# Cross-shaped window attention on one core: a newly searched instruction order, three integer and two product buffers, and a start that loads half of x transposed

## The chip, the core and the metric

The kernel runs on one core of a Trainium2 chip. The metric is the device time of one execution in microseconds. TensorE (PE; PEld is its weight load), VectorE (DVE), ScalarE (ACT), GpSimd (POOL) and SyncE (SP) each work through their own list of instructions in order and wait for each other through semaphores.

## What is computed

```python
def reference(x, wqkv, wo):            # x 1x224x224x96, wqkv 96x288, wo 96x96
    qkv = jnp.einsum('bhwc,cd->bhwd', x, wqkv)      # q, k, v: 96 channels each
    # channels 0..47: 28 horizontal stripes of 8 rows x 224 columns = 1792 tokens
    ah = _softmax(jnp.einsum('bqc,bkc->bqk', qh, kh) * scale, axis=-1)
    oh = jnp.einsum('bqk,bkc->bqc', ah, vh)
    # channels 48..95: 28 vertical stripes of 8 columns x 224 rows, the same
    ...
    return jnp.einsum('bhwc,cd->bhwd', o, wo)       # o: both halves side by side
```

So there are 56 attention problems of 1,792 queries by 1,792 keys with 48 channels, and a projection before and behind them.

## The kernel before, in words

**Tiling.** The kernel treats two stripes at a time (a band, `P`, 28 of them: 14 horizontal, then 14 vertical). The two stripes sit side by side in the partitions of TensorE's operands. The 1,792 queries are cut in chunks of 512, 512, 512 and 256 (`CH`). A unit is one chunk against 128 keys (256 for the short chunk), for both stripes: a pair of score matmuls that run at once (L988) fills two PSUM banks with 128 x 1024 scores.

**Two ways to an exponential.** Of the 1,372 units, 1,092 go through ScalarE's Exp, PSUM to a bf16 tile `PT` (L1010). The other 280 (4, 2, 2, 2 a band by chunk, `NDC`) go through integers: VectorE adds a constant and rounds the scores to int16 (`I_sb`, L1048). Two such units make a pair: VectorE masks the pair's fraction into `U_sb` (L1060) and its exponent into `E_sb` (L1062), and the product of `I_sb` and `U_sb`, read as bf16, goes to `G_sb` (L1066). The sum E + G stands for the exponential, so TensorE multiplies both with V. A product of 512 columns is made on POOL, one of 1,024 on VectorE; a bit of the string `far` says which for each half of a pair. Buffers for I and U: `NY` = 2 pairs, for E and G: `NL` = 3 pairs (L396).

**Rest of a band.** TensorE multiplies PT, E and G with V (L941) into one bank per chunk; VectorE copies the finished chunk to `OT_sb` (L904); TensorE multiplies it with wo and a column of ones (L793, L829); VectorE divides by the sums. Horizontal results are staged and moved by DMA to `Ph_sb`, which stays in SBUF; POOL adds vertical results to it (L842), and a DMA writes the output. In between, "fills" make the next band's Q, K (L679) and V (L744) from `xT_sb`, x with channels in the partitions, which transposing DMAs on SP load two bands ahead (`load`, L556).

**What sets the order.** A planner inside the kernel (`Planner`) keeps streams of operations for each engine. It takes the next operation of TensorE, VectorE and POOL from the strings in `PLAN`, a digit for the stream: on TensorE 0 start, 1 scores for ScalarE, 2 scores for VectorE, 3 values times E or G, 4 values times PT, 5 final projection, 6 fill. `bank` gives the PSUM banks. The planner's assumed durations (`ACT` and `SWITCH` at L161 and L162, the numbers handed to `Op` and `fill`) place operations against each other in time, choose free buffers and order SP. They are no instructions; the chip sees only the order and the waits.

**Start.** For band 0, x of both stripes is loaded as plain rows, 112 partitions of 16 tokens (L496; one DMA on SP, one on ACT), turned by 32 matmuls against an identity (`x_turn`, L645) and copied to `xT_sb` (L650). The tokens come out permuted, so the first Q is read in that order (L674) and its copies from PSUM undo it in two strided pieces each (L690, L692). `NWARM` = 6 matmuls on zeros run before that (L524), three more (`warmer`, L757) between the first fills.

Of the kernel before, what the change touches and what calls it, by code (L numbers as in the profile page):

```python
# [24 lines left out]
NDC = [4, 2, 2, 2]  # L25

# [3 lines left out]
        "00000000000000000006000611602106162164144116444123316446121443163124144124143314613413413312416441261341163441"  # L30
        "36312514412316123144414412614411333544146153124164124133361123443134126413411644541135445441441241331241641136"
        "44416451451611333531241644113644125414412414414126133312514414614341612331351241631431341264143116444411464453"
        "13312514412416341154441135443634161541631251431241644112644414412313411344441254134121613331241641341334124164"
        "11354441144544614613313612441541231531144446313641611354451241361612441461241441331241434124154134144125133135"
        "16412316441331641241364116443441213341541245144113644411464464161133344153412514312416412614414412313411364441"
        "44615412316123315314123414312316431164444116445441631313541241631246144115344411633441412631441153461245144124"
        "14414412613331251441461431641233136154123143134126413411644441146543313155414412613412461441136441133444124613"
        "41154461235144124144144126133312514414614316412331361215341431341264134116444411464431335124164145135124414611"
        "36444113344614512315441231612416414414331241341241441631441463135123164144123313441126443146114345414412413314"
        "61244163114644531144361351541236144513126144126144144124154411333541213441441251331234151344133124164113644416"  # L40
        "46146133123514412415311464461134443113464461351241541136446121444126144144412315312315413414441215313312614413"
        "64133121644411364444116446413313451541241631246144113644113344461531241541234164112444164412313311444421451431"
        "21633136124163143153144126341441163444116345315412461441251341134444113364461311544541236144126144126144144123"
        "13411433451241441233154135164123164133412416411364444116444613313412541412431541146344114334611544531612431641"
        "26141241644144123134113455414416412331341261341241531334124164631461411344446155144133124164312416411344441133"
        "54451143641261341261412461441441231341134544124154132133134125144146133136124163114464431461231341146446124135"
        "41146434114633514411364451241354124164121644144121334113344412416412416213313613413312461441135444114464451541"
        "64133135123416412461341154444114633115446344121543412416124164115444213134125133144144126133312416413413314612"
        "44163116445431541214441146444123163411643441154461541336135124413312416124164115444441213313514413461241641233"
        "13164123144313412641341164454113644514414441231631246144114334411633511446345124153412164124164144412133411354"  # L50
        "44124164133134126314412614313314641251341146445415414413413312614412361441163454414133411644612351441531241612"
        "41444164121333154124163144146313125414412413313341241641136444146416413312316412451441136444115446133113544441"
        "26313412614412614414412313411345441241641333141263144126134133412416411364431145334615414124514412316441136444"
        "11463311544541634125134412164124164115444213134125313414414126133312416413413341241641136444114644541631331543"
        "14126414312641441164441331154464515312316124154412414414412613341251331441441136346123415412316413341261441164"
        "44311346335154141246144125134114364441146331154464312514412316412614411444434121353144123144162161333154124163"
        "12461441331541146343114463351544141264144123614411354441143344611164453354124161241541241441641213331541231441"
        "44126313312614416312414363144116444113345331645145144164123145124316411544441163316412531441231641261441154444"
        "12415412335313441116444463312415412416431341361341254133146114644415412441331412641341164454316115444123341641"
        "16345124154312414414123134121633144144126313411644331146335124164311544641531241612514414412416411464453133161"  # L60
        "13544413316441153444126131241644115444412153134125133124144124153131241354431441154444123153135411354415412451"
        "4441125441331145443113544412415414412331541144413341334115434354455"),
    "dve": (
        "00000000000000000003333333332332344323343232442444413232344133233244232344313333232144232333333314423323443333"
        "33313323323442312344333213233442323443333132332334343331333323323442324142133234423234434333333132332344333133"
        "33323324432214432132333334432323344123332334433331332332344232441333321323442323443333331332323443331233332344"
        "23123443332132334423234433313333332323443123333234423123443332132344233234433313323333323443133323323442321442"
        "31333244232333134423323344331333332333234423233144233123344233234433333123323334433133323333244231233442133233"
        "34423234433331333323234431333233244323244132132334432332334431333332323443313333323234423241442133233333442323"
        "44333312332334431333333232344232144333332123442332333314433333232344133333232344232144332132344333232344313233"  # L70
        "32334433331333233234423244412321344232334433333333133232344331333323323234412334442313234423323333331234432344"
        "33333313342323234434123344332132444232333333134432324443133333323323442321443332123442333233333344413232334413"
        "33323333244321323344231323444232344333312323344333314332323442321443332123442323344433331332332344313333332332"
        "32344312344423132344232344333333413323234431433333332323442312344423313323344232334443333133232334431333323323"
        "24431423443213323323443233344433331332323443413333333232344321324443231233244323344433333313332332344313332332"
        "32344343213323344313233444323343233134432323333134433233332344212344423123444333323333333213234323434343433413"
        "433432323443413233243234123434323443432333431333323344323434313342343233444144333313333"),
    "pool": (
        "00000000022122222222222222222222122222222222222222222122222222222222222222212222222222222222212222222222222222"
        "22221222222222222222222221222222222222222222221222222222222222222221222222222222222222222122222222222222222221"  # L80
        "22222222222222222222122222222222222222212222222222222222222212222222222222222222221222222233332222222221222223"
        "32222333332222222222133222222333332222332222132232222333222222222231322223222233322222233222212222223333222222"
        "22223122223222233333222222222212233322333322322223223122223222233332222223322122223223333322322223221222233222"
        "233332233223221332222332222322322322221333333322333333333333332233333"),
    "far": (
        "01001111111111111111111111111111111011111111111111111111111111111111111111111111111111111111111111111111111111"
        "11111111011111111111111111111111111111101111111101111111010110110111111110111111011111011111101111101111011001"
        "110111110111101110101101111110011011110101110000100000000100"),
    "bank": (
        "76547654760127665502475044275047205420540135025320530530404603643064316042064260426426042605326513651365230636"  # L90
# [281 lines left out]
def bass_standalone__window_attn_cswin__vision_kernel(  # L372
# [29 lines left out]
    with es:  # L402
# [234 lines left out]
        def x_cols(c0, c1):  # L637
            return [x_evs[(w, g)] for g in range(4) for w in range(2) if c0 < 4 * XP * (g + 1) and c1 > 4 * XP * g]
# [387 lines left out]
        def add_d(u, soft):  # L1026
# [26 lines left out]
            if j == 0:  # L1053
                return
# [141 lines left out]
```

## Time and profile before

| | us |
|---|---|
| time, median of 3 runs (1023.18 to 1023.66) | 1023.42 |
| profiled execution, its own time | 1023.4 |
| its span, first to last instruction | 1021.6 |
| first exponential starts | 12.32 |
| last exponential ends | 1015.68 |
| busy: TensorE, VectorE, ScalarE, GpSimd | 1001.8, 914.6, 1008.2, 677.6 |

The profile is one execution. Its page gives busy time of each engine, the chain of work that ended last (followed back from the end, at each step to what released it), and groups of instructions with a count, busy time, mean duration and the idle time before them. Matmuls and exponentials are pipelined: one starts before the last has ended, so busy time is a union and the distance from start to start says more than a duration. The timeline lists instructions in order of time, merged where equal ones follow each other, with idle time and its releaser in brackets.

### The profile page before, as it was taken

To read this page: it belongs to the slowest core of one execution; us is meant where nothing else is said; L and a number is where in the kernel's file an instruction comes from. 1 tells how busy PE (TensorE), PEld (TensorE's weight loads), DVE (VectorE), ACT (ScalarE), POOL (GpSimd) and SP (SyncE) were. 2 spreads that over 40 slices of the span, in tenths; PEclk is the share of its full clock that TensorE was granted. 3 is DMA by queue.
4 is the path that set the end of the run, shared out by engine and by line. 5 is a ranking of instruction groups with operands and counts; after the bars stand their busy time and mean duration, and the time that the engine had idled before them with its cause. 6 is when DMAs were issued, how large, how long until landed. Compare 5 with 4: busy or idle time off the path is not lost.

```text
span 1021.6 us, 25550 instructions
## 1 busy us (share of the span) xinstructions
PE 1001.8 (98%) x10681; PEld 387.9 (38%) x10681; DVE 914.6 (90%) x1660; ACT 1008.2 (99%) x1106; POOL 677.6 (66%) x623
## 2 busy tenths in 40 slices
PE   8999999999999999999999999999999999999997
PEld 3333333333333334334333333333333333333333
DVE  8989989988988998898889889989889999998998
ACT  7999999999999999999999999999999999999997
POOL 2667657667756757665677776777677676676534
PEclk9999999999999999999999999999999999999999
DMA  4122443141244342331432212112212222221012
GB/s 103 38 26 41 64 51 42 37 64 29 43 59 48 46 63 39 28 56 31 49 58 47 43 36 56 40 38 45 47 41 42 49 44 46 51 51 33 22 29 48
DMA packets 187915, 46.49 MB, mean 46 GB/s; under 512 B 187576, under 2 KB 187576, under 8 KB 187800
## 3 DMA queue, kind: packets, MB, share of 16 engines
q1 hardware_dynamic: 187432, 44.44, 26.8%
q8 instruction: 83, 1.36, 0.6%
q10 hardware_dynamic: 368, 0.43, 0.1%
q14 instruction: 32, 0.26, 0.1%
HBM read 0.79 MB, written 9.63 MB: 10 GB/s over the span
## 4 chain that ended last, share of the span: by engine, by line
ACT 96%; PE 3%; DMA 0%; DVE 0%; issue 0%; DVEq 0%
ACT PT L1010 96%; PE ps L941 1%; PE ps L988 1%; DMA Ph_sb<-in_x_dram 0%; PE ps L679 0%; PE ps L645 0%; PE ps L829 0%; PE ps L744 0%; DVE out_sb L861 0%; PE ps L757 0%; DVE OT_sb L904 0%; DVE rc L834 0%; PE ps L793 0%; DVEq L402 0%; DVE tmp L838 0%
## 5 line engine op out<-in xcount | busy, mean ns | idle before, releaser
L1010 ACT ACTIVATE PT<-ps 128x1024 bf16<-128x1024 f32 x1092 | 1002.4, 1168 | 1.4 <-PE ps L988 1.0
L1066 POOL TENSOR_TENSOR G_sb<-I_sb,U_sb 128x512 bf16<-128x512 bf16 x472 | 531.3, 1155 | 294.2 <-DVE E_sb L1062 272.5
L988 PE MATMUL ps<-QT_sb,KT_sb 48*128 48x512 bf16 (+1 forms) x3136 | 464.5, 356 | 10.3 <-ACT PT L1010 3.6
L1048 DVE TENSOR_SCALAR I_sb<-ps 128x1024 int16<-128x1024 f32 x280 | 341.6, 1220 | 27.3 <-PE ps L988 21.8
L941 PE MATMUL ps<-PT,V_sb 128*64 128x512 bf16 (+1 forms) x2464 | 364.7, 362 | 0.4 <-ACT PT L1010 0.3
L988 PEld LDWEIGHTS ps<-QT_sb,KT_sb 48*128 48x128 bf16 x3136 | 123.4, 93 | 312.6 <-ACT PT L1010 247.5
L941 PEld LDWEIGHTS ps<-PT,V_sb 128*64 128x64 bf16 x2464 | 118.9, 109 | 113.5 <-issue 90.5
L842 POOL TENSOR_TENSOR out_sb<-tmp,Ph_sb 112x384 bf16<-112x384 f32 x111 | 99.2, 913 | 31.5 <-DVE G_sb L1066 13.8
L941 PE MATMUL ps<-G_sb,V_sb 128*64 128x512 bf16 (+1 forms) x672 | 108.5, 354 | 0.1
L1060 DVE TENSOR_SCALAR U_sb<-I_sb 128x2048 int16<-128x2048 int16 x140 | 99.4, 710 | 0.3
L941 PE MATMUL ps<-E_sb,V_sb 128*64 128x512 bf16 (+1 forms) x672 | 96.2, 354 | 0.8 <-DVE OT_sb L904 0.2
L1062 DVE TENSOR_SCALAR E_sb<-I_sb 128x2048 int16<-128x2048 int16 x140 | 96.4, 688 | 0.0
L679 PE MATMUL ps<-xT_sb,w_sb 96*64 96x512 bf16 x448 | 83.3, 372 | 0.2
L904 DVE CAST OT_sb<-ps 128x512 bf16<-128x512 f32 x112 | 69.6, 621 | 14.5 <-PE ps L941 13.3
L699 DVE TENSOR_SCALAR QT_sb<-ps 128x512 bf16<-128x512 f32 x108 | 66.7, 620 | 16.0 <-PE ps L679 15.3
L705 DVE TENSOR_SCALAR_CACHE_REDUCE KT_sb<-ps 128x512 bf16<-128x512 f32 x110 | 67.7, 619 | 8.4 <-PE ps L679 7.9
L749 DVE CAST V_sb<-ps 128x480 bf16<-128x480 f32 (+1 forms) x112 | 55.8, 501 | 9.5 <-PE ps L744 9.1
L838 DVE TENSOR_TENSOR tmp<-ps,rc 112x384 f32<-112x384 f32 x111 | 61.6, 555 | 2.9 <-DVE rc L834 0.2
L717 POOL TENSOR_SCALAR KT_sb<-KT_sb,negmean 128x1792 bf16<-128x1792 bf16 x27 | 47.5, 1761 | 14.9 <-DVE E_sb L1062 10.9
L800 DVE TENSOR_TENSOR out_sb<-ps,rc 128x384 bf16<-128x384 f32 x98 | 54.5, 556 | 2.9
L941 PEld LDWEIGHTS ps<-G_sb,V_sb 128*64 128x64 bf16 x672 | 34.2, 108 | 44.0 <-issue 32.6
L744 PEld LDWEIGHTS ps<-w_sb,xT_sb 96*64 96x64 bf16 x1568 | 35.9, 112 | 25.9 <-issue 10.0
(45 smaller groups left out, 337.0 us busy)
## 6 DMA issues: line engine op xcount, KB each, us to landing
Ph_sb<-out_sb SPq DMA_DIRECT2D x112, 84.0 KB, 4.4
out_dram<-out_sb SPq DMA_DIRECT2D x111, 84.0 KB, 1.9
xT_sb<-in_x_dram SPq DMA_TRANSPOSE x250, 2.5
Ph_sb<-in_x_dram SPq DMA_DIRECT2D x1, 336.0 KB, 4.7
Ph_sb<-in_x_dram ACTq DMA_DIRECT2D x1, 336.0 KB, 4.9
out_dram<-out_sb ACTq DMA_DIRECT2D x1, 84.0 KB, 2.1
wo_sb<-in_wo_dram SPq DMA_DIRECT2D x4, 9.0 KB
wo_sb<-one_sb SPq DMA_DIRECT2D x4, 0.0 KB
```

What stands on the lines that cost most here:

```text
L679: ins = e.matmul(bk[64 * w:64 * w + 64, 0:qs], lhsT=w_sb[0:C, wblk(P, kind), :], rhs=rhs, start=True, stop=True)
L699: return e.tensor_scalar(dst, src, A128, None, ALU.mult)
L705: return e.tensor_scalar(dst, src, 1.0, None, ALU.mult, ALU.add, accum_out=acc)
L842: return e.tensor_tensor(out_sb[b][0:HB, :, w, 2 * c:2 * c + 2, :].rearrange("p h d c -> p d h c"), tmp[hold[1].tok["t"]][0:HB, 0:n, :].re ...
L904: return e.tensor_copy(OT_sb[b][:, q0:q0 + qs], bk[:, 0:qs])
L941: return e.matmul(bank(k.bank)[64 * w:64 * w + 64, x0:x1], lhsT=lhs(w, kts[i])[p0:p1], rhs=rhs(w, i, qs)[p0:p1, x0:x1], start=(op.tok["fir ...
L988: ins = e.matmul(bank(op.tok["s"][w])[:, i * qs:(i + 1) * qs], lhsT=KT_sb[b][64 * w:64 * w + C2, kt * 128:(kt + 1) * 128], rhs=QT_sb[b][64 ...
L1010: a.fn = lambda e: e.activation(PT[a.tok["p"]][:].rearrange("p (s n) -> p s n", s=2), two(q.tok["s"]), ACTF.Exp, scale=LN128)
L1048: return e.tensor_scalar(dst[:, at:at + 1024].rearrange("p (s n) -> p s n", s=2), two(src), 128.0 * ONE, 0.0, ALU.add, ALU.max)
L1060: f.fn = lambda e: e.tensor_scalar(U_sb[y()][:, :], I_sb[y()][:, :], M_FRAC, HALF, ALU.bitwise_and, ALU.bitwise_or)
L1062: x2.fn = lambda e: e.tensor_scalar(E_sb[x2.tok["l"]][:, :], I_sb[y()][:, :], M_EXP, E_LOW, ALU.bitwise_and, ALU.bitwise_or)
L1066: g.fn = lambda e: e.tensor_tensor(G_sb[x2.tok["l"]][:, i0:i1], I_sb[y()][:, i0:i1].bitcast(BF16), U_sb[y()][:, i0:i1].bitcast(BF16), ALU. ...
```

## The change

The strings of `PLAN` are replaced by others found in a new search; two assumed switch times, the exponential's and several operations' assumed durations change. The pool of integer buffers grows from 2 to 3 pairs and that of products shrinks from 3 to 2. At the start the first stripe's x comes by a transposing DMA on SP straight into `xT_sb`; the second stripe's comes as rows on ACT's queue and is turned by 16 matmuls, whose copies now write the natural order of tokens, so the first Q's copies are plain. All K and Q fills of band 0 wait for both. The weight load moves from SP to ACT's queue. The warm-up matmuls ahead become 9, and two more warmers stand between turning and K. A table of counts by band (`NDP`) is added, empty, and a last unit without a partner could be treated alone.

```diff
@@ planner's figures @@
-SWITCH = {"q": 0.122, "v": 0.097}
-ACT = 0.9165
+SWITCH = {"q": 0.096, "v": 0.097}
+ACT = 0.904
...
-    NPT, NY, NL, NR = 8, 2, 3, 4
-    NWARM, EARLY = 6, 256
+    NPT, NY, NL, NR = 8, 3, 2, 4
+    NWARM, EARLY = 9, 256
...
-        for w in range(2):
-            src = bass.AP(x.tensor, x.offset + w * NTOK * C, [[XJ * C, XP], [1, XJ * C]])
-            op = Op("sp" if w == 0 else "act", 0.65, 3.0, lambda e, w=w, src=src: e.dma_start(xn[0:XP, w, :], src), dma=(s_nat[w], 0))
...
+        x_nat = Op("act", 0.45, 4.1, lambda e: e.dma_start(xn[0:XP, :], src), dma=(s_nat, 0))
+        q_first["act"].append(x_nat)
+        x_tr = Op("sp", 1.3, 5.1, lambda e: e.dma_start_transpose(xT_sb[0][:, 0:1, :], bass.AP(x.tensor, x.offset, [[C, NTOK], [1, 128]])),
+                  dma=(s_x[0][0], 0))
+        q_first["sp"].append(x_tr)
...
-        op_w0 = Op("sp", 0.7, 2.8, lambda e: e.dma_start(w_sb[0:C, :, 0:C2], wqkv.rearrange("c (s d) -> c s d", s=6)), [o_w0], dma=(s_w0, 0))
-        q_first["sp"].append(op_w0)
+        op_w0 = Op("act", 0.7, 3.6, lambda e: e.dma_start(w_sb[0:C, :, 0:C2], wqkv.rearrange("c (s d) -> c s d", s=6)), [o_w0], dma=(s_w0, 0))
+        q_first["act"].append(op_w0)
...
@@ x_turn @@
-                dst, src = xT_sb[0][0:C, w, 4 * g * XP:4 * (g + 1) * XP], bk[0:C, 0:4 * XP]
+                dst = xT_sb[0][0:C, 1, :].rearrange("c (p j) -> c j p", j=XJ)[:, 4 * g:4 * g + 4, :]
+                src = bk[0:C, 0:4 * XP].rearrange("c (j p) -> c j p", j=4)
...
-                on_act = startup and (c < 2 if kind == "q" else c % 2)
+                on_act = startup and (c < 1 if kind == "q" else c % 2)
...
-                    xs = x_cols(0, NTOK) if kind == "q" else x_cols(q0, q0 + qs)
+                    xs = [x_tr] + x_evs
...
-                p, ops = fill(0.43 * qs / 1024, pe_fn, xs + [op_w0], evs, ...
+                p, ops = fill(0.025 + 0.43 * qs / 1024, pe_fn, xs + [op_w0], evs, ...
...
-                p, ops = fill(0.045 * n, pe_fn, (x_cols(k0 * 128, (k0 + n) * 128) if startup else [x_op[(P, w)]]) + [op_w0, o_v1],
+                p, ops = fill(0.0335 * n, pe_fn, ((x_evs if w else [x_tr]) if startup else [x_op[(P, w)]]) + [op_w0, o_v1],
...
-                work = [(t, w, g) for g in range(4) for w in range(2)] + [(k, "k", c) for c in range(NCH)] + [
+                work = [(t, g) for g in range(4)] + [(f, 0), (f, 1)] + [(k, "k", c) for c in range(NCH)] + [
...
```

Of the strings, TensorE's begins with 25 start codes in a row where it began with 19, then a fill and three more. It has 1,092, 280, 560, 1,092, 210 and 329 of the codes 1 to 6, as before; `far` has 242 ones of 280 where it had 236; POOL's has 484 products where it had 472.

## The prediction

> **What bounds the kernel now.** I began with the page. Its first lines show two full engines, its fourth part the chain that ends last, its fifth the groups.
>
> ```profile
> span 1021.6 us, 25550 instructions
> PE 1001.8 (98%) x10681; PEld 387.9 (38%) x10681; DVE 914.6 (90%) x1660; ACT 1008.2 (99%) x1106; POOL 677.6 (66%) x623
> ACT 96%; PE 3%; DMA 0%; DVE 0%; issue 0%; DVEq 0%
> L1010 ACT ACTIVATE PT<-ps 128x1024 bf16<-128x1024 f32 x1092 | 1002.4, 1168 | 1.4 <-PE ps L988 1.0
> L1066 POOL TENSOR_TENSOR G_sb<-I_sb,U_sb 128x512 bf16<-128x512 bf16 x472 | 531.3, 1155 | 294.2 <-DVE E_sb L1062 272.5
> L1060 DVE TENSOR_SCALAR U_sb<-I_sb 128x2048 int16<-128x2048 int16 x140 | 99.4, 710 | 0.3
> L1062 DVE TENSOR_SCALAR E_sb<-I_sb 128x2048 int16<-128x2048 int16 x140 | 96.4, 688 | 0.0
> ```
>
> The reader sees a stream of 1,092 exponentials that carries 96% of the chain, with only 1.4 us of idle in front of them. That hides the real loss, because successive exponentials overlap (1,168 ns each, 1,002 us together). So next I read their starts in the trace: 796 of the 1,091 distances are 904 or 905 ns, the mean is 918.5. **904 ns is the pace of a fed ScalarE; (918.5 - 904) x 1,091 = 15.8 us is lost to scores that come late.** Of it 11.3 us lie in 79 distances over 960 ns, and it is spread evenly: 1.1 to 1.7 us in each 100 us, 2.7 in 900 to 1000.
>
> Then the chain in order of time, for the two ends:
>
> ```profile
> 0.74 4.66 DMA Ph_sb<-in_x_dram
> 5.44 3.22 PE ps L645 x32
> 8.66 1.99 PE ps L679 x8
> ...
> 11.96 0.34 PE ps L988 x2
> 12.32 360.63 ACT PT L1010 x393
> ...
> 988.07 27.61 ACT PT L1010 x30
> ```
>
> The first exponential starts at 12.32 and the last ends at 988.07 + 27.61 = 1015.68. The row of 393 has a pitch of 360.63 / 393 = 0.918.
>
> Last, one stall in the timeline, and the waits:
>
> ```profile
> 906.36 0.63 PE L941 MATMUL ps<-E_sb,V_sb 128*64 128x256 bf16 x8 [0.20 <-ACT PT L1010]
> 906.82 0.34 PE L829 MATMUL ps<-wo_sb,OT_sb 128*64 128x97 bf16 x8
> 906.99 0.38 PE L941 MATMUL ps<-G_sb,V_sb 128*64 128x256 bf16 x4
> 907.31 0.39 PE L988 MATMUL ps<-QT_sb,KT_sb 48*128 48x512 bf16 x2
> 907.74 1.02 ACT L1010 ACTIVATE PT<-ps 128x1024 bf16<-128x1024 f32 x1 [0.52 <-PE ps L988]
> ```
>
> ```profile
> PEld ps L988 <- ACT PT L1010: 247.5, 728, 0.8
> DVE I_sb L1048 <- POOL G_sb L1066: 1.6, 2, 0.9
> ```
>
> The exponential waits because the written order put other matmuls ahead of its scores, not because TensorE has too much to do: score matmuls wait for ScalarE to free a bank 728 times.
>
> **The sum's frame.** Profiled time 1023.4 = 1.8 around the span + 12.32 to the first exponential + 1,091 x 0.904 = 986.3 + 15.8 of stalls + 1.27 (the last exponential) + 5.92 (its end to the span's end). The median shown is 1023.42, the same. The change can touch 12.32, 15.8 and 5.92 only: the number of exponentials (code 1, 1,092 times in both strings) stays.
>
> **Part 1, the start.** Removed: 16 of 32 turning matmuls, 93 ns apart, 1.49 us; four of eight evictions. Moved: the rows now go out on ACT's queue, whose transfer of the same size landed at 5.69, not the 5.40 at which SP's did. So turning runs from 5.73 to 7.22. The first K fill now needs all four turned groups. The fourth group's last matmul starts at 7.13; its eviction on ACT follows as before after 0.335 and takes 0.54: 8.00, so K starts at about 8.06, not 8.59 (two new warm-ups, 2 x 0.427 from 7.22, fill this wait). The transposing DMA of the other half sits first on SP: the first such transfer here took 5.55 from issue to landing, so 0.74 + 5.55 = 6.3, behind cover. At the late end it lands at 7.7, as the first one does now, and still hides. Ahead of it on SP the row transfer goes away; behind it the two transposes for the second band slide by about a microsecond at most and have until 14 us. The weight load moves to ACT's queue behind the rows and ahead of the table load: issued at about 1.4, and at SP's 4.6 us it lands near 6.0, before 8.06; the 1.28 us table load slides by some 0.7 into time when ACT idles until 6.46.
>
> From the first K fill to the first score took 11.89 - 8.59 = 3.30. Its string now holds all 25 start codes ahead of the first score: behind q come warm-up, V, warm-up, V, warm-up with pitches 0.38, 0.32, 0.43, 0.32, 0.43, and 0.32 to the score, 2.20, on top of 1.325 from K to q. That is 3.53: first score at 11.59, first exponential 0.43 later, 12.02, a gain of 0.30. At this part PE's pace matters: matmuls of 512 columns stand 427 ns apart until about 9.5 us and 213 to 225 later (the granted-clock column reads 1.00 throughout, so the pitches are what tells). The warm-up grows from 6 to 9 (9 x 0.427 from 1.19 reaches 5.03), so the idle stretch shrinks from 1.5 us to under 1. If PE is at its fast pace by 5.7, turning saves 0.75 and the fills 0.6 more; then the evictions (2.75 from K to the corrected keys) bind, and the exponential comes at 10.7. The other bound is a late strided eviction or weight load: 13.3. The strided eviction itself is priced by L690, 0.39 for 256 strided columns, against 0.38 for dense ones on L704: nothing. I take 11.7, nearest to the 12.02, so **-0.6**.
>
> The Trainium skill, "TensorE: Matmul & The Clock Gate", section "What's actually happening", says that about 3.4 us of sustained work in a free-running window releases the full clock. The trace's switch near 9.5, 4.1 us after work resumed at 5.44, fits it. By the rule alone the 3.84 us of warm-up may or may not do it, and the start would be 10.7 or 12.0.
>
> **Part 2, the order of the stream.** Count the strings. Both have 1,372 score pairs (codes 1, 2), 1,652 value products (3, 4), 210 finals (5), 329 fills (6). The switches between score and value work rise from 1,838 to 1,915. By pitches in the trace: 0.2165 per score pair, 0.226 per value product, 0.17 a final, 0.208 a fill, 0.098 a switch (305 to 312 instead of 213): 954.6 us before, 962.2 after. Per exponential 0.874 and 0.881, both under 0.904. So 77 switches cost 7.5 us of TensorE, covered as long as TensorE has 22 us to spare.
>
> Why then 15.8 of stalls? The order was laid out for an exponential every 0.9165 (ACT, L162) with a switch of 0.122 to scores and 0.045 per V block. The chip runs at 0.904, so ScalarE outruns the order by 0.0125 x 1,091 = 13.6 us, and has to be stopped for it; what is left, 2.2, is the order's own. The new string is laid out for 0.904, a switch of 0.096 and V blocks of 0.0335, which are what the trace measures (93 to 104 ns; 0.030 to 0.034). So the 13.6 can go. It won't go whole: the hidden margin between planned and real TensorE work sinks from some 37 us (992 by the old figures against 955) to 10 (972 against 962), so a wait that used to be swallowed now reaches ScalarE. Bounds for the stalls: 2.2 and 15.8. I take **6**, in the half nearer to 2.2, since the 13.6 has a cause that goes: **-9.8**.
>
> **Part 3, products and buffers.** far has 242 ones for 236: six halves move from DVE (0.695 each, -4.2 us of 914.6) to POOL (12 x 1.155 = +13.9 of 677.6). Neither engine is full. From the write of E to the last read of its pair takes 6.8 us in the middle and 11.3 at most; two buffers would have been free at least 2.8 us before their next use, so the third product buffer did nothing: 0. The integer pair lives 10.6, at most 16.5, and two buffers came free 0.1 to 0.7 us ahead in the tight places, with the 1.6 us of waits shown above; a third takes these away. DVE is not on the chain, so I count 0 and leave the gain in the 6.
>
> **Part 4, the rest.** The end: behind the last score the new string has two value products, then two finals at the very end as before: 5.92 stays. The empty table of counts and the case of a lone unit do nothing (ten units in each band, always paired). Sum: 1.8 + 11.7 + 986.3 + 6 + 1.27 + 5.92 = **1013.0**.
>
> **Rivals.**
> *Stalls come back elsewhere.* TensorE has less slack, and where 25 exponentials in a row hold over 0.904 of its work each (4% of stretches before, 9% after) they stall anyway; only the start gains. Stalls 15 to 17: 1022 to 1024, say 1023. For it: even now PE is at 98%. Against: no stretch of 100 exceeds 0.90.
>
> *Slower: products arrive late on POOL.* Place: the G reads in TensorE's queue, which end only 1.25 us (median) after the last product; behind them wait the next scores. U's operation takes 661 to 695 ns alone, but up to 1,321 where a POOL operation lies beside it (25 of 140 have one). With more on POOL in a shorter span (691 + 99 + 96 + 26 = 912 of 986 us, against 904 of 1002) such meetings multiply. TensorE's slack is 7.8 exponentials x 0.023 = 0.18 us a pair; a pair late by more than 0.30 eats the whole gain ((0.30 - 0.18) x 140 = 17). At 0.35: 1007 + 24 = 1031. Against: TensorE waited for POOL's products only 3.9 us, 13 times.
>
> The Trainium skill, "SBUF — State Buffer", section "SBUF: two separate sides", says that DVE in a two-port mode and GpSimd exclude each other for a whole instruction. The stretched U rows agree; the rule speaks for this rival.
>
> *The search reaches the floor.* Stalls of 2 and an early clock: 1.8 + 10.7 + 986.3 + 2 + 7.2 = 1008.
>
> **How the numbers follow.** The forecast, 1009 to 1019, 0.62; no net gain in the stream (1020 to 1025) 0.14; late products (1026 to 1040) 0.17; the floor (under 1009) 0.07. What a measurement can tell from no change is 0.2%, 1021.4 to 1025.5. Half of the second case counts as the same: faster 0.75, same 0.08, slower 0.17. The range 1007.5 to 1024 leaves out the third case and little else.
>
> **What would show it.** The distances of exponentials: mean about 0.9095 (stalls 6), the 904 unchanged; the first exponential at 11.7; the end 5.9 after the last. DVE's wait for POOL's G_sb ahead of I_sb gone; no wait ahead of E_sb. Wrong if TensorE's waits for G_sb grow past 25 us, if the 904 itself moves, or if the transposing load becomes the release of the first K fill.

## The result, and the profile after

| | before | after |
|---|---|---|
| time, median, us | 1023.30 (4 runs) | 1034.93 (4 runs, 1034.64 to 1034.99) |
| profiled span | 1021.6 | 1033.1 |
| first exponential starts | 12.32 | 15.85 |
| first start to last end of the exponentials | 1003.35 | 1011.34 |
| last end to the span's end | 5.92 | 5.92 |

The ratio is 1.0113, 95% interval 1.0095 to 1.013: slower by 11.6 us (11.5 in the span), where 10 us less was forecast. The ratios given with the runs below are not those of the medians: ten of the 66 executions of the kernel before that were taken beside those runs, and four of the twelve with the buffers alone, lasted 1028.5 to 1030.1 us (no trace of one was kept), which moves a ratio by up to 0.0015. The page of the changed kernel shows where to look.

```profile
span 1033.1 us, 25551 instructions
PE 1015.9 (98%) x10670; PEld 389.6 (38%) x10670; DVE 915.9 (89%) x1651; ACT 1010.2 (98%) x1101; POOL 690.2 (67%) x635
PEclk6799999999999999999999999999999999999999
ACT 93%; PE 6%; DVE 0%; issue 0%; DVEq 0%
L1002 ACT ACTIVATE PT<-ps 128x1024 bf16<-128x1024 f32 x1092 | 1003.1, 1171 | 11.2 <-PE ps L980 10.8
```

The reader sees three things. TensorE's share of the chain has doubled from 3% to 6%. The idle time in front of the exponentials is 11.2 us, not 1.4. And the row of the granted clock, full in every slice before, starts with 6 and 7: TensorE did not have its full clock in the first 50 us. The chain in order of time shows the start of it.

```profile
1.19 4.02 PE ps L529 x9
5.21 0.76 PE ps L647 x8
6.00 3.95 ACT xT_sb L653 x2
10.19 2.13 PE ps L680 x10
...
69.14 958.06 ACT PT L1002 x1045
```

Between the turning (L647) and the first K fill (L680) stand two copies from PSUM to `xT_sb` on ScalarE, 3.95 us. Before, the DMA, the turning and the fills followed each other with nothing of the sort between them. The view of these copies by line, minimum, median and maximum in ns:

```profile
L653 DVE CAST xT_sb<-ps x2: 2076/2146/2217, 5.6 to 7.3; 96x448 bf16<-96x448 f32 x2
L653 ACT ACTIVATE xT_sb<-ps x2: 2076/2212/2349, 6.0 to 7.6; 96x448 bf16<-96x448 f32 x2
```

The kernel before has the same copies, of the same size, at 620 and 540 ns (L650). Those of the changed kernel write each element 32 bytes from the last. The strided copies of the kernel before (L690, 256 columns) are the ones that the prediction took its price from:

```profile
L650 DVE CAST xT_sb<-ps x4: 620/621/621, 6.1 to 8.3; 96x448 bf16<-96x448 f32 x4
L650 ACT ACTIVATE xT_sb<-ps x4: 540/541/541, 6.5 to 8.7; 96x448 bf16<-96x448 f32 x4
L690 ACT ACTIVATE QT_sb<-ps x4: 384/399/415, 10.6 to 11.4; 128x256 bf16<-128x256 f32 x4
```

Then the stretches of the changed kernel's start: span, then busy time and number of instructions of PE, PEld, DVE, ACT and POOL, the granted clock, and the DMA engines' share and rate. The clock column begins to tell with the first rise, here at 6.68; before it, it reads 1.00 although the matmuls stand 427 ns apart:

```profile
5.00:10.10 5.10, 2.19 (x19) 1.65 (x17) 3.94 (x2) 3.94 (x2) 0.00 (x0) 1.00 1.03 201
10.10:25.00 14.90, 14.46 (x106) 4.75 (x107) 9.59 (x19) 8.72 (x12) 1.90 (x2) 0.50 0.01 1
25.00:40.80 15.80, 15.80 (x66) 3.14 (x62) 8.72 (x16) 10.24 (x10) 6.58 (x6) 0.50 0.30 58
40.80:56.00 15.20, 15.18 (x174) 5.79 (x172) 13.16 (x21) 14.87 (x17) 10.54 (x10) 1.00 0.01 3
```

While the copies run, TensorE idles 3.0 us (7.19 to 10.19). At 10.10 its clock falls to half and stays there for 30.7 us, although TensorE is busy nearly all of them: exponentials stand up to 1.96 us apart, because the score matmuls and what stands between them take twice as long. Only from 40.8 on is the stream what the new order was made for.

### The profile page after: what moved, and what is told of

Read it like the earlier page. It is cut to its first block, busy times and chain, and to the rows that moved or that the text cites. A ratio compares the mean times of both kernels' runs of the same rounds, so it can differ in the third digit from the quotient of the medians.

```text
span 1033.1 us, 25551 instructions
## 1 busy us (share of the span) xinstructions
PE 1015.9 (98%) x10670; PEld 389.6 (38%) x10670; DVE 915.9 (89%) x1651; ACT 1010.2 (98%) x1101; POOL 690.2 (67%) x635
## 3 DMA queue, kind: packets, MB, share of 16 engines
q1 hardware_dynamic: 188536, 44.49, 27.3%
## 4 chain that ended last, share of the span: by engine, by line
ACT 93%; PE 6%; DVE 0%; issue 0%; DVEq 0%
ACT PT L1002 93%; PE ps L980 2%; PE ps L933 2%; PE ps L680 1%; PE ps L529 0%; ACT xT_sb L653 0%; PE ps L736 0%; PE ps L749 0%; PE ps L785 0%; DVE out_sb L853 0%; PE ps L647 0%; DVE OT_sb L896 0%; PE ps L821 0%; DVE rc L826 0%; DVE warm L504 0%
## 5 line engine op out<-in xcount | busy, mean ns | idle before, releaser
L1002 ACT ACTIVATE PT<-ps 128x1024 bf16<-128x1024 f32 x1092 | 1003.1, 1171 | 11.2 <-PE ps L980 10.8
L1059 POOL TENSOR_TENSOR G_sb<-I_sb,U_sb 128x512 bf16<-128x512 bf16 x484 | 544.3, 1154 | 311.0 <-DVE E_sb L1055 302.1
L980 PE MATMUL ps<-QT_sb,KT_sb 48*128 48x512 bf16 (+1 forms) x3136 | 473.9, 359 | 6.7 <-ACT PT L1002 3.8
L933 PE MATMUL ps<-PT,V_sb 128*64 128x512 bf16 (+1 forms) x2464 | 386.4, 367 | 0.6 <-ACT PT L1002 0.5
L933 PE MATMUL ps<-E_sb,V_sb 128*64 128x512 bf16 (+1 forms) x672 | 100.9, 353 | 0.2
L680 PE MATMUL ps<-xT_sb,w_sb 96*64 96x512 bf16 x448 | 84.0, 379 | 3.2 <-ACT xT_sb L653 3.0
L691 DVE TENSOR_SCALAR QT_sb<-ps 128x512 bf16<-128x512 f32 (+1 forms) x111 | 67.7, 619 | 11.6 <-PE ps L680 11.0
L741 DVE CAST V_sb<-ps 128x480 bf16<-128x480 f32 (+1 forms) x112 | 55.8, 501 | 12.4 <-PE ps L736 11.8
```

Source lines behind the costliest of these rows:

```text
L680: ins = e.matmul(bk[64 * w:64 * w + 64, 0:qs], lhsT=w_sb[0:C, wblk(P, kind), :], rhs=rhs, start=True, stop=True)
L691: return e.tensor_scalar(dst, src, A128, None, ALU.mult)
L933: return e.matmul(bank(k.bank)[64 * w:64 * w + 64, x0:x1], lhsT=lhs(w, kts[i])[p0:p1], rhs=rhs(w, i, qs)[p0:p1, x0:x1], start=(op.tok["fir ...
L980: ins = e.matmul(bank(op.tok["s"][w])[:, i * qs:(i + 1) * qs], lhsT=KT_sb[b][64 * w:64 * w + C2, kt * 128:(kt + 1) * 128], rhs=QT_sb[b][64 ...
L1002: a.fn = lambda e: e.activation(PT[a.tok["p"]][:].rearrange("p (s n) -> p s n", s=2), two(q.tok["s"]), ACTF.Exp, scale=LN128)
L1059: g.fn = lambda e: e.tensor_tensor(G_sb[x2.tok["l"]][:, i0:i1], I_sb[y()][:, i0:i1].bitcast(BF16), U_sb[y()][:, i0:i1].bitcast(BF16), ALU. ...
```

## The experiments

One theory and two rivals stood at first. **Theory:** the slow copies make the loss, by a late start and by the idle stretch that costs the clock. **Rivals:** the new order starves the exponentials in its first 40 us by itself; or the longer warm-up brings the half clock whatever the copies do.

### Dense copies

```diff
-                dst = xT_sb[0][0:C, 1, :].rearrange("c (p j) -> c j p", j=XJ)[:, 4 * g:4 * g + 4, :]
-                src = bk[0:C, 0:4 * XP].rearrange("c (j p) -> c j p", j=4)
+                dst, src = xT_sb[0][0:C, 1, 4 * g * XP:4 * (g + 1) * XP], bk[0:C, 0:4 * XP]
...
+                        if kind == "q" and startup and w == 1:
+                            rhs = xT_sb[b][0:C, w, :].rearrange("c (j g q) -> c g q j", j=XJ, g=SW)[:, :, q0 // 128:(q0 + qs) // 128, :]
```

> The changed kernel, but the turned half of x is copied from PSUM in a dense row again (permuted tokens), and the first Q is read for that stripe in the permuted order; keys and values of one stripe share the permutation, so nothing else changes. Theory (the copies that write every 16th element take 2.1 to 2.3 us instead of 0.54 to 0.62, TensorE idles 3 us behind them and its clock falls to half for 31 us): copies back at 0.54 to 0.62, first exponential at 10.8 to 11.5 instead of 15.85, no half-clock stretch in the stream, the 9.9 us of stalls before 41 us gone, time 1019 to 1021.5. Rival 1 (the new order itself starves the exponentials in its first 40 us): first exponential early, but 8 us or more of stalls before 41 us stay, time 1029 or more. Rival 2 (the longer warm-up brings the half clock whatever the copies do): copies short, half clock still there, time 1028 or more.

Measured: 1022.18 us, 0.9982 of the kernel before (0.9968 to 0.9996). The first exponential starts at 10.71 and the long half-clock stretch is gone. The copies:

```profile
L652 DVE CAST xT_sb<-ps x2: 611/616/620, 5.2 to 5.8; 96x448 bf16<-96x448 f32 x2
L652 ACT ACTIVATE xT_sb<-ps x2: 531/535/539, 5.4 to 5.9; 96x448 bf16<-96x448 f32 x2
```

Both rivals fall: with the new order and the longer warm-up in place, neither a starved first 40 us nor a long half clock is left. The time is 0.7 us above the expected range, for a reason of the same kind: now the first Q is read with a stride, and three matmuls of 512 columns take 1,097 to 1,107 ns instead of 379. With these in the way the clock fell once more, for a single 3.4 us (14.85 to 18.27), and 2.5 us of exponentials were lost before 20 us.

### The idle stretch filled, the copies left slow

```diff
-                work = [(t, g) for g in range(4)] + [(f, 0), (f, 1)] + [(k, "k", c) for c in range(NCH)] + [
+                work = [(t, g) for g in range(4)] + [(f, 0)] * 16 + [(k, "k", c) for c in range(NCH)] + [
```

(and 14 more start codes and banks in the strings)

> The changed kernel with its slow strided copies, and 14 more matmuls on zeros between the turning and the first K fill, which cover TensorE's idle 3 us. Theory (the idle stretch alone takes the clock away): copies still 2.1 to 2.3 us, K fills still near 10.2, but at full clock from there on: first exponential at 13 to 13.8, stalls before 41 us under 1 us, time 1021.5 to 1024. Rival 1 (order): 1031 to 1035. Rival 2 (clock falls for another reason): half clock stays, 1033 to 1036.

Measured: 1022.89 us, 1.0001 of the kernel before (0.9979 to 1.0023). The copies still take 2,060 to 2,371 ns, yet in the profiled execution the clock is full in every stretch:

```profile
5.00:10.10 5.10, 4.70 (x36) 2.50 (x36) 3.96 (x2) 3.96 (x2) 0.00 (x0) 1.00 0.97 191
10.10:25.00 14.90, 13.83 (x144) 5.00 (x143) 14.13 (x29) 13.31 (x18) 4.49 (x4) 1.00 0.32 63
```

One of the ten executions took 1032.90 us at a mean clock of 0.989 (0.999 in the profiled one), so the filling did not keep the clock in every execution; no trace of that one was kept.

So the idle stretch alone cost the clock, and the clock cost the larger part. With it full, the stream takes 1001.60 us from first start to last end; in the changed kernel it took 1011.34. That splits the loss in the span: 15.85 - 12.32 = **3.53 late start, 1011.34 - 1001.60 = 9.74 half clock, 1001.60 - 1003.35 = -1.75 new order**, together the 11.5. The clock has a share in the late start too: with the filling the first exponential starts at 13.23, only 0.91 later than in the kernel before, although the copies are as slow. The profiled executions of the changed kernel and of this run, 1034.90 and 1022.54 us, lie 12.4 us apart, and nearly all of that is the lost clock's. The slow copies by themselves only ate the gain: the best start below reaches 9.91.

### A shorter filling

The same with 5 matmuls on zeros instead of 14.

> As the run before, with 5 more matmuls instead of 14, so that TensorE idles about 2 us instead of 3. The theory leaves open how long an idle stretch takes the clock away: if 2 us are not enough, the time is as with 14, 1021.5 to 1024; if they are, the half clock comes back for some 30 us and the time is 1032 to 1035.

Measured: 1032.78 us, in a single execution. TensorE idles 2.31 us (7.20 to 9.51) and the half clock comes back, from 11.27 for 27.3 us. The stretches, read as above:

```profile
11.20:25.00 13.80, 12.98 (x95) 3.73 (x92) 9.38 (x18) 8.89 (x11) 3.98 (x4) 0.50 0.16 35
25.00:38.50 13.50, 13.50 (x56) 2.60 (x53) 7.49 (x15) 8.90 (x9) 4.49 (x4) 0.50 0.20 34
```

So 2.3 us of idling can be enough here. In the kernel before, 1.5 us of idling (3.93 to 5.44) lay in a start that had not reached the full clock yet; it came at 9.73.

### The buffers alone

```diff
-    NPT, NY, NL, NR = 8, 2, 3, 4
+    NPT, NY, NL, NR = 8, 3, 2, 4
```

in the kernel before.

> The kernel before, old order and old start, with three integer and two product buffers. Theory (two product buffers were free 2.8 us before their next use at the least, three integer buffers only take away 1.6 us of waits on VectorE, which is not on the chain): 1022 to 1023.6, no change that can be told. Rival (the smaller product pool makes E wait for TensorE's reads): over 1025, with a wait of E_sb on PE in the waits.

Measured: 1023.60 us, 1.0018 of the kernel before (0.9998 to 1.0037). The stream takes 1003.35, as before to the hundredth, and no wait of E's operation on TensorE appears. The buffers do nothing that can be told.

### Dense copies without a strided read

```diff
-        src = bass.AP(x.tensor, x.offset + NTOK * C, [[XJ * C, XP], [1, XJ * C]])
+        src = bass.AP(x.tensor, x.offset + NTOK * C, [[C, XP], [XP * C, XJ], [1, C]])
...
-                dst = xT_sb[0][0:C, 1, :].rearrange("c (p j) -> c j p", j=XJ)[:, 4 * g:4 * g + 4, :]
+                dst, src = xT_sb[0][0:C, 1, 4 * g * XP:4 * (g + 1) * XP], bk[0:C, 0:4 * XP]
...
-    NWARM, EARLY = 9, 256
+    NWARM, EARLY = 14, 256
```

> The changed kernel, with the turned stripe's rows loaded so that partition p holds tokens p, p+112, p+224 and so on (pieces of 192 bytes instead of 3,072). The copies from PSUM are then dense and the tokens in natural order, so neither a copy nor the first Q needs a stride. 14 warm-ups instead of 9 cover the wait for the rows. Theory (strides cost the start, the rest of the new order is worth some 2 us): copies 0.54 to 0.62, first Q fills at the usual pace, first exponential at 10.3 to 11.3, no half clock in the stream, stalls 13.5 to 14.5, time 1019 to 1020.8. Rival (small pieces make the rows land after 7 us): first exponential near 12, 1021 to 1022.

Measured: 1021.38 us, 0.9975 of the kernel before (0.9962 to 0.9987). No stride, no half clock. But the first exponential came at 12.16: TensorE stayed at the slow pace until 6.8 in this run, so 14 warm-ups lasted until 7.0, while the rows had landed at 4.73. The rival (late rows) falls; what went wrong is the longer warm-up, which held the turning back.

### What holds the stream: TensorE's work, or products that come late

One question was left. The prediction took 9.8 us off the stream for the new order, and the runs show 1.75; the distances between starts still add up to 14.0 us over 904 each. So I took work away. In the first two runs TensorE multiplies only 64 columns of E with V, each time or every sixth time:

```diff
-                        ins = mm(e, i, w, 0, 0, qs, 0, 128)
+                        ins = mm(e, i, w, 0, 0, 64 if cut and not op.tok["first"] and k.last is not op else qs, 0, 128)
```

> As the run with 14 fillers, and TensorE multiplies only 64 of the columns of E with V from the second band on (first and last product of a chunk kept whole), some 49 us less of its work in the same order; the output lacks those products. Theory A (scores are late because TensorE, at 97% of the pace of the exponentials, has too little room to catch up): stalls past 41 us fall from 13.7 to under 5, time 1011 to 1015. Theory B (scores are late because of waits on VectorE or POOL in front of TensorE's list): stalls stay over 10, time over 1019.

> The same with every sixth of those products cut, about 8 us of TensorE's work, the price of the 77 added switches. Theory A in proportion: stalls past 41 us fall by 1.5 to 3 us, to 10.7 to 12.2. Theory A with a threshold (the margin of the order before is what counts): by more than 4. Theory B: by less than 0.7.

And in a third the products on POOL and VectorE are cut to 64 columns:

```diff
+                i1 = i1 if units[0][0] < 2 else i0 + 64
                 g.fn = lambda e: e.tensor_tensor(G_sb[x2.tok["l"]][:, i0:i1], ...
```

> As the run with 14 fillers, and from the third band on each product of I and U, on POOL and VectorE alike, is made for 64 columns only (the other columns of G hold old values, so the output is not the reference's). TensorE's work is the same, but G is there several us early and POOL hardly uses the port it shares with VectorE. Theory A (TensorE's own work): stalls past 41 us stay at 11 to 14, time 1020 to 1023. Theory B (late products, or U's operation stretched beside POOL): stalls fall under 7, time 1012 to 1016.

Measured: 1022.80, 1022.56 and 1022.54 us, against 1022.54 for the profiled run with 14 fillers. Each of the three was executed once. **Nothing moved, and both theories fall**, A by the first two runs and B by the third. TensorE's busy time on the products of E fell from 99.9 to 60.1 us in the first and to 91.9 in the second, POOL's busy time from 690 to 313 in the third, and the distances behind the 60th exponential still add up to 12.95 to 12.97 us over 904 in all four runs. In the first of them the single late starts lie elsewhere (those of 60 to 140 ns fall from 57 to 44, those over 140 rise from 14 to 21), and the sum is the same. Something else pins it.

The trace says what, when one reads ends instead of starts. In a row of exponentials started 904 ns apart, each takes some 12.5 ns longer than the last: 1,088, 1,100, 1,113, 1,126, 1,138, 1,150 (from 196.8 us on, in the run with 14 warm-ups and dense copies). So the ends stand 916.7 apart. The starts run ahead of the engine's work until a start lies up to about 1,340 ns ahead of its end, or until scores are a little late; then they fall back. From the 60th exponential on, the end pitch in the changed kernel lies between 912 and 937 without one exception, with a mean of 916.7. In the kernel before, 11 ends in the same part are late, by 2.0 us in all. **So ScalarE was full nearly all along, and 916.7, not 904, is its pace;** the next two runs test it. The chain of waits had said so before any experiment: its row of 393 exponentials has a pitch of 0.918, with no break.

### The new theory tested: a shorter exponential

From the second band on, each exponential leaves out the last columns of each bank.

```diff
+            m = 512 if P < 1 else 512 - 8      # second run: 512 - 32
+            a.fn = lambda e: e.activation(PT[a.tok["p"]][:].rearrange("p (s n) -> p s n", s=2)[:, :, 0:m], two(q.tok["s"])[:, :, 0:m], ACTF.Exp, scale=LN128)
```

> The same, and from the second band on each exponential leaves out 16 of its 1,024 columns (the last 8 of each bank; the output then holds old values there). New theory (the true pace is 916.7 a piece, the distances over 904 between starts only pay back what ScalarE's queue had run ahead): 0.83 ns a column by the difference between exponentials and copies of other widths, 13.3 ns each, so 1,053 x 13.3 = 14.0 us less: time 1005 to 1007, end pitch near 903. First theory, as in the prediction (904 is the pace, the rest is scores that come late): what is late stays late, 1017 or more.

> The same with 64 columns left out (32 of each bank), 56 us less of ScalarE's work if nothing else held. What comes next is the question: TensorE's work adds up to 962 us and some 12 of start and end, so the time flattens. Expected 985 to 1003, and end pitches no longer even. If it falls the full 56 us (under 968), TensorE has more room than its pitches say.

With 16 columns less: 1009.00 us, and the end pitch is 903. The stream is 11.2 us shorter than the 1001.6. That is under the 14.0 expected, and the time 2 us above the range, for three reasons in the trace: the clock fell for one stretch of 3.4 us (13.88 to 17.29) and cost 1.5 us, about 1.4 us went to 31 late ends behind the 60th exponential, and the first exponential came at 10.89, 1.0 us later than in the whole kernel with the same start (9.91, below). The prediction's reading (nothing gained) falls. With 64 columns less: 1004.71 us, a stream of 986.1, with the same 3.4 us of half clock in its start; the time is 1.7 us above the expected range. Both runs were executed once. Now ScalarE no longer carries the chain. Two lines of the page, then the chain by line, with 64 columns out:

```profile
span 1002.9 us, 25550 instructions
PE 993.1 (99%) x10669; PEld 388.9 (39%) x10670; DVE 910.5 (91%) x1651; ACT 978.3 (98%) x1101; POOL 690.7 (69%) x635
by line: PE ps L932 42.9%; PE ps L979 38.7%; PE ps L679 5.7%; PE ps L735 3.0%; PE ps L820 2.4%; PE ps L784 2.1%; DVE I_sb L1040 1.0%; ACT PT L1002 0.9%; PE ps L529 0.4%; issue 0.4%; DVE E_sb L1055 0.3%; POOL out_sb L833 0.3%; DVE tmp L829 0
```

TensorE has the chain and ScalarE 0.9% of it. So the next bound, with this order, is TensorE at about 986 us (1.5 of them the clock's), 1.5% under ScalarE's 1001.6.

### The best start, and the old order with it

The run with the rows in pieces, with 9 warm-ups:

> The kernel with 192-byte pieces and dense copies again, with the change's 9 warm-ups instead of 14 (14 reached 7.0 us at the slow pace, 2 us after the rows had landed at 4.7). New theory: the ends of exponentials stand 916.7 ns apart from one end of the stream to the other, so ScalarE is full and only the start is left to gain. First exponential 10.2 to 11.0, stream (first start to last end) 1001.6 as in the runs before, time 1019.2 to 1020.5. Rival (the short idle stretches of the start lose the clock again): 1021 or more, with a half-clock stretch behind 10 us.

Measured: **1019.33 us, 0.9954 of the kernel before (0.9937 to 0.9972)**, the fastest of the kernels that leave nothing out. The first exponential starts at 9.91 (a little before the expected range), the stream takes 1001.59.

```profile
53.46 958.06 ACT PT L1001 x1045
```

This chain row has the same 958.06 us for 1,045 exponentials as that of the changed kernel: the stream does not feel what the start was. The rival did not happen in this profile; in the two runs with shorter exponentials, which begin alike, it did, for 3.4 us.

The same start with the strings and buffers of the kernel before (start codes adapted):

> The order and the buffers of the kernel before, with the start of the first run here (rows in pieces, dense copies, transposing load, 9 warm-ups). It parts order from start. New theory: the old order loses 2.0 us to 11 late exponentials and the new one nothing, so the stream takes 1003.4 to 1003.7 instead of 1001.6, time 1.7 to 2.3 us above the first run of this call. By the prediction's step the new order is worth 9.8 us: 7 or more above it.

Measured: 1021.27 us, 0.9967 of the kernel before (0.9949 to 0.9985), 1.94 above the run before; the stream takes 1003.35. Its chain is cut where the old order starves ScalarE; the first four rows of the stream:

```profile
9.98 367.05 ACT PT L1001 x400
378.05 107.36 ACT PT L1001 x117
485.43 359.59 ACT PT L1001 x392
856.97 21.20 ACT PT L1001 x23
```

So, by the traces, the order is worth 1.8 us (1003.35 to 1001.59), and the start, done without strides, 2.3 to 2.4 (12.32 to 9.98 and 9.91).

## Why the prediction was wrong, point by point

- **The strided copies were priced at nothing, and that decided the sign.** The row used for it, L690, writes runs of eight elements (16 bytes) and costs 0.38 to 0.42 us, about as much as a dense copy. The change writes single elements, 32 bytes apart: 2.08 to 2.35 us instead of 0.54 to 0.62. The row was near in its name ("strided") and not in what it does. So K started at 10.19 and not at the 8.06 of Part 1, although the rows landed at 4.14, sooner than the 5.69 of the sum. The Trainium skill, "SBUF — State Buffer", section "Door 1: The DMA port swizzle", states that the memory has lines of 16 bytes and that each access which goes on to a new line pays; the two rows agree with it, and it would have told them apart.
- **The clock was weighed for what an earlier rise might gain, not for what a fall would cost.** The idle stretch that the prediction named, between the warm-up and the turning, did go: nine matmuls last until 5.21, and the turning follows. The one that cost the clock lies behind the turning. The prediction saw it too, and let two warm-up matmuls fill it at the slow pace; with the slow copies 3.0 us of it stayed empty, behind a clock that had already risen. No term of the sum is a fall of the clock. It cost 9.74 us in the stream, and the start came out at 15.85, outside the 10.7 to 13.3 given for it.
- **"904 ns is the pace of a fed ScalarE" was false.** It is the distance of starts while the queue runs ahead; the pace is 916.7. So of the 15.8 us of stalls 13.6 were the distance between 904 and the true pace, and 2.2 were late ends (2.0 behind the 60th exponential, 0.2 before it). The new order could give 2.2 at the most, where 9.8 was forecast; it gave 1.75, because it loses some 0.46 in its own first 60. The old assumed figure in the kernel, 0.9165, was right, and the new one, 0.904, harmless. The step "the 13.6 has a cause that goes" had the planner's figure to blame for what was the engine's own pace.
- **The switches and TensorE's margin:** 77 more switches cost nothing that shows, as said: taking 40 us off TensorE's products of E changed nothing.
- **The rival of late products did not happen.** TensorE waited for POOL's products 4.1 us (3.9 before), and products of 64 columns brought nothing. The slower result came by a mechanism that the prediction didn't list.
- **Right:** the buffers (0), the transposing load (landed at 5.93, hidden), the weight load (6.48, hidden), the end (5.92), the six halves moved to POOL.

## What to carry to other kernels

The pace of a pipelined engine shows in the distance between ends, or in a long unbroken row of the chain divided by its count; the distance between starts can show how far its queue runs ahead instead. What settles it is to take work off that engine and off the others: here only the first shortened the stream. When a change puts a copy on the path of the start, look for a row with the same run of bytes, not one that is merely strided, and ask how long TensorE idles behind it. An idle stretch of 3.0 us behind a risen clock cost some 12 us here, and matmuls on zeros in it won them back in nine of ten executions.

## What the runs showed of the hardware that was not expected

- Once the clock had fallen it stayed at half for 30.7 us behind 3.0 us of idling and for 27.3 us behind 2.3 us, with TensorE over 94% busy in these stretches; in three runs (the first with dense copies and the two with shorter exponentials) it fell for 3.4 us, with TensorE idle only in pieces of 0.2 to 0.45 us before. Such pieces alone do not decide it: the best start has the same ones and kept the clock. All of these lengths are whole multiples of 3.41 us, and so are the stretches of full clock ahead of them (3.41 in the changed kernel, 6.83 with 5 fillers). The Trainium skill, "TensorE: Matmul & The Clock Gate", section "What's actually happening", has the full clock come after at least one busy window, with about 3.4 us of sustained work as the time for it. The window's length agrees; the return took eight and nine windows here, and one in the three other runs. What ends the half clock is open; no run tried it.
- A moving operand read with 224 bytes between elements made a matmul of 512 columns take 1,097 to 1,107 ns instead of 379.
- The full clock came between 4.1 and 7.1 us in the eleven profiled runs that begin with the same 9 warm-ups (at 6.7 in the changed kernel). The number of warm-up matmuls that suffices is not fixed.
- An exponential of 1,024 columns holds ScalarE for 916.7 ns, one of 1,008 for 903. The Trainium skill, "ScalarE: Activation LUTs", section "What ACT_TABLE_LOAD costs", gives 186 ns and 0.833 a column where scale and bias are immediates, less 93 of overlap between neighbours: an estimate of 946 by that page. The slope nearly agrees (13.7 / 16 = 0.86); with the page's slope the fixed part of the 916.7 is an estimated 64, where the page's figures leave 93.
